# ScalarE copies the finished accumulators out of PSUM, and a memset moves ahead of the first values

## The chip, the cores and the metric

The kernel runs on one core of a Trainium2 chip. The core has a matrix engine (TensorE, PE in the profile, with its weight loads as PEld), three engines for elementwise work (VectorE or DVE, ScalarE or ACT, GpSimd or POOL) and a queue that issues most transfers (SyncE, SP). The metric is the device time of one execution in microseconds (us), of which the median over several runs counts.

## The reference

The input `x` has 8 batches of 3072 rows and 256 columns. The reference takes the Fourier transform over rows and columns, keeps the real part and sends each of the 24576 rows through a small two-layer network:

```
h = real(fft2(x)) @ w_in          # 256 -> 2048
g = max(h, 0) + alpha * min(h, 0) # alpha: one value per hidden unit
y = g @ w_out                     # 2048 -> 256
```

## The kernel before, in words

The transform uses symmetries, so that each batch gives two families of values, kept in a tile `X` of four rows of 1552 columns: row 0 and row 1 hold the high and the low part of one family, rows 2 and 3 those of the other. The functions `unit_store` and `to_x` write `X` (line 592: ACT writes the high part; line 593: POOL or DVE the low part). The buffer of `X` is used earlier in the run by a tile `before`, for input pieces and weights.

The network then works on 26 blocks of columns of `X` (`BLOCKS`, line 28): four of width 386 or 384, eighteen of width 512, four of 386. Each block has 16 steps, one for each 128 hidden units, so there are 416 steps, numbered `s`. `step(s)` (line 795) does, in program order:

- `ffn1(s + 3)`: six first-layer matmuls for the step three ahead, into two of four PSUM banks of the pool `pq`;
- `ffn2(s)`: the second-layer matmuls of this step, twelve once the start is over, into four accumulator banks `acc[o, i]`. `o` is the half of the 256 output columns, `i` one of the two rows that come from one pair of values. The pool `accp` has one buffer for each of the four, so the next block uses the same banks;
- in the last step of a block, `evacuate(g, 0)`: the two banks of half 0 are copied to SBUF and stored;
- `pair(s + 3)`: the activation. DVE adds (`sums`, `row`), ACT makes the product with alpha (line 714), DVE takes the maximum (line 666), ACT rounds to the high part (`hi`, line 668), POOL subtracts for the low part (`lo`, line 670);
- in the last step of a block, `evacuate(g, 1)`: the same for half 1.

The order of `ffn2`'s matmuls is written out. In the last step of a block (line 758) all of half 0 comes first. In all others (line 760) it is half 0 with `woh`, half 0 with `wol`, then half 1 with `wol`, and so on, each for both `i`.

The order of work is written by hand: each engine executes its instructions in the order of the program, and semaphores are set where one instruction needs the result or the place of another. In the first block the steps also prepare the weights (`weights_f`, `weights_b`, `weights_m` on POOL, `weights_mm` on PE), and beside the later steps the transforms and folds of the next batch are made. Input pieces are loaded on SP's queue into a ring of four buffers (`load`, line 186), each as soon as the piece four places ahead of it in the list is used up (`fold_whole`, line 428).

Seven columns behind the last value of `X` are set to zero by a memset on POOL (line 911), after step 3.

Of the kernel before, what the change touches and what calls it, by code (L numbers as in the profile page):

```python
# [9 lines left out]
F32 = mybir.dt.float32  # L10
# [15 lines left out]
XS, X0 = 1552, 7  # L26
SINGLE = 1537
BLOCKS = [(0, 0, 386), (0, 386, 384), (0, 770, 384), (0, 1154, 384)]
# [10 lines left out]
def _halves(v):  # L39

    return v.rearrange("p (h a) -> p a h", h=2)


def _pairs(v):

    return v.rearrange("p (a h) -> p a h", h=2)
# [85 lines left out]
def fft2_prelu_ffn(ctx: ExitStack, tc: tile.TileContext, t, outputs):  # L132
# [17 lines left out]
    V, S, G = nc.vector, nc.scalar, nc.gpsimd  # L150
# [7 lines left out]
    zres = small.tile([P, P], F32, name="zres")  # L158
    before = xp.tile([P, 4, XS], F32, tag="X", name="before")
    dummy = work.tile([P, 512], F32R, tag="hi0", name="dummy", bufs=3)  # L160
# [121 lines left out]
    def weights_m(f, e):  # L282
        a, m = wpart.pop(f)
        w = st.tile([P, 512], F32, tag="w32", name="w32", bufs=2)
        e.tensor_tensor(out=w.bitcast(I32), in0=a, in1=m, op=ALU.add)  # L285
        w32[f] = w
# [239 lines left out]
    def dft(kind, half, fe, fo, zr, m, bank=None):  # L526

        ps = (bank or other_bank())[0:m]
        if kind in TABS:
            tab = TABS[kind]  # L530
            n = 193 if kind[1:] == "ee" else 192
            o = 0 if kind[1:] == "ee" else 3
            even = [(fe[:, o], tab[:, 0]), (fe[:, o + 1], tab[:, 1])]
            if kind == "cee":
                even.append((zr, ee[:, 4]))
            oddp = [(fe[:, o + 1], tab[:, 2]), (fe[:, o + 2], tab[:, 3])]
        else:
            n = 192
            sl = slice(half * 192, (half + 1) * 192)
            even = [(fo[:, q], odd[:, q, sl]) for q in range(3)]  # L540
            oddp = [(fo[:, 3 + q], odd[:, 3 + q, sl]) for q in range(3)]
        for o, terms in ((0, even), (n, oddp)):
            for i, (lhsT, rhs) in enumerate(terms):
                nc.tensor.matmul(  # L544
                    out=ps[:, o:o + n], lhsT=lhsT, rhs=rhs, start=(i == 0), stop=(i == len(terms) - 1),
                )
        return ps, n, m
# [23 lines left out]
    def unit_mm(b, kind, half, bank=None):  # L571
        s = 0 if kind[0] == "c" else 2
        fe, fo = (fold[b, "ce"], fold[b, "co"]) if s == 0 else (fold[b, "se"], fold[b, "so"])
        return dft(kind, half, fe, fo, zres, P, bank)

    def unit_store(b, kind, half, lo_engine, y):
# [9 lines left out]
        if kind == "cee" and 0 < b < NB - 1:  # L586
            c = X0 + SINGLE + b
            lo_engine.tensor_copy(out=X[:, 0:2, c:c + 1], in_=X[:, 0:2, X0:X0 + 1].bitcast(F32))

    def to_x(s, c, v, lo_engine):  # L590
        hi, lo = (X[:, s + i, X0 + c:X0 + c + v.shape[-1]] for i in range(2))
        S.activation(out=hi, in_=v, func=ACTF.Copy)  # L592
        lo_engine.tensor_tensor(out=lo, in0=v, in1=hi.bitcast(F32), op=ALU.subtract)  # L593
# [41 lines left out]
    def column_128_store(kind, y):  # L635
        at, n = _place(1, kind), 385 if kind == "cee" else 384
        nc.sync.dma_start(out=xcd[1:NB, at:at + n], in_=y[1:NB, 0:n])
        at, n = _place(0, kind), y.shape[-1]
        nc.sync.dma_start(out=xcd[0:1, at:at + n], in_=y[0:1])
        if kind == "cee":  # L640
            nc.sync.dma_start(
                out=xcd[NB - 1:NB, SINGLE:SINGLE + 7].rearrange("o (b k) -> (o b) k", k=1), in_=y[0:NB - 1, 0:1],
            )
# [31 lines left out]
    def ffn1(s):  # L675
# [4 lines left out]
        for q in range(2):  # L680
            t_ = pq.tile([P, 512], F32, tag="pq", name="pq")[:, 0:w]
            xh, xl = X[:, 2 * q, c:c + w], X[:, 2 * q + 1, c:c + w]
            xh, xl, out = _halves(xh), _halves(xl), _pairs(t_)
# [54 lines left out]
    acc = {}  # L738
# [34 lines left out]
    def evacuate(g, o):  # L773
        b, c, w = BLOCKS[g]
        if o == 0:
            outs[g] = outp.tile([P, 2, 2, w], F32, tag="o", name="o")
        v = outs[g]
        dst = outputs[g]
        for i in range(2):
            if o == 0:  # L780
                S.activation(out=v[:, o, i], in_=acc[o, i], func=ACTF.Copy)
            else:
                V.tensor_copy(out=v[:, o, i], in_=acc[o, i])
        nc.sync.dma_start(out=dst[:, o], in_=v[:, o])

    outs = {}
# [8 lines left out]
    def step(s):  # L795

        g, f = divmod(s, KF)

        def on(fn, f_, *a):
            if 0 <= f_ < KF:  # L800
                fn(f_, *a)

        if 0 <= s + LEAD < NSTEP:
            ffn1(s + LEAD)
        if s >= 0:
            ffn2(s)
            if f == KF - 1:
                evacuate(g, 0)
        on(weights_mm, s + AHEAD + 1)
        on(weights_ih, s + AHEAD)  # L810

        def early():
            on(weights_c, s + AHEAD)

        def late():
            on(weights_f, s + AHEAD + 3)
            on(weights_b, s + AHEAD + 2)
            on(weights_m, s + AHEAD + 2, G)
            on(weights_out, s + AHEAD + 1)

        if s + LEAD <= NSTEP:
            pair(s + LEAD, early, late)
        if s >= 0 and f == KF - 1:
            evacuate(g, 1)
        for f_ in SPLITS.get(s, ()):
            weights_split(f_)
# [28 lines left out]
    weights_b(1)  # L855
    weights_m(1, G)
    X = xp.tile([P, 4, XS], F32R, tag="X", name="X")
    see_sums = unit_mm(0, "see", 0)
    cee_sums = unit_mm(0, "cee", 0)
    x_sums = odd_sums(*x_sums)  # L860
# [40 lines left out]
    for b in range(NB):  # L901
        mine = [g for g, block in enumerate(BLOCKS) if block[0] == b]
        r_odd, r_fold, r_end = (16, 16, 50) if b == 0 else (0, 4, 36)
        beside = []
        for r in range(len(mine) * KF):
            s = mine[0] * KF + r
            g, f = divmod(s, KF)
            step(s)
            if b == 0:
                if r == 3:  # L910
                    G.memset(X[:, :, X0 + SINGLE:X0 + SINGLE + 7].bitcast(F32), 0.0)  # L911
                    nc.sync.dma_start(out=odd, in_=t["odd"])
                if r == 9:
                    column_128_store("ceo", butterfly(*column_128_mm("ceo", 0)))
                if r in (10, 11):
                    unit(0, ("ceo", "seo")[r - 10], 0, G)
                if r in (12, 13):
                    fold_cross(0, ("co", "so")[r - 12])
                    if r == 13:
                        fold_128(0)  # L920
                if r == 25:
                    start.close()
                    late = ctx.enter_context(tc.tile_pool(name="late", bufs=1))
                if r in TABLE_STEPS:
                    q = TABLE_STEPS.index(r)
                    v = late.tile([P, 1, 384], F32, tag="table", name="table", bufs=2)
                    nc.sync.dma_start(out=v, in_=t["odd"][:, q:q + 1])
                    parts(v, "odd", G, q)
            if f == 10:
                load_xbc(g + 1)  # L930
            q = r - r_odd
            if b == 0 and q in (0, 2, 4, 6):
                unit(b, ("co", "so")[q // 2 % 2], q // 4, G)
            if b and q in (0, 3):
                nm = ("co", "so")[q // 3]
                store_odd(b, nm, dft_odd(b, nm), G)
            if b + 1 < NB:
                if r == r_fold:
                    fold_tiles(b + 1)
                for i, e, r0, r1 in FOLDS:  # L940
                    r0, r1 = (r_fold + round(v * (r_end - r_fold)) for v in (r0, r1))
                    if r == r0:
                        by = one_by_one if e is V else spread
                        beside.append(by(fold_whole(6 * b + 6 + i, e), r0, r1))
                for x in beside:
                    next(x, None)
                if r == r_end + 1:
                    fold_rows(b + 1)
                    fold_cross(b + 1)
                    fold_128(b + 1)  # L950
                for nm, at in (("co", 60), ("so", 62)) if b == 0 else (("co", 44), ("so", 46)):
                    if r == at:
                        parts(fold[b + 1, nm], nm, G)
                for kind, at in zip(("see", "cee", "ceo", "seo"), (53, 55, 57, 58) if b == 0 else (38, 40, 41, 42)):
                    if r == at:
                        unit(b + 1, kind, 0, G)
# [64 lines left out]
```

## Time and profile before

| What | us |
|---|---|
| median of 3 runs (lowest, highest) | 1664.68 (1663.48, 1667.77) |
| the profiled execution | 1664.33 |
| its span in the profile | 1662.5 |
| busy: PE, DVE, POOL, ACT | 1642.7, 1473.8, 1299.3, 1123.8 |
| PE's share of the chain that ended last | 93% |

A busy time says how long an engine executed something. The chain that ended last is followed back from the last instruction, at each step to what released it. In the rows of a timeline the first number is the start in us from the span's start, the second the duration of the merged group, then come engine, line, operation, tiles and the number of instructions; in brackets stands the engine's idle time just before, and what ended it.

### The profile page before, as it was taken

The numbers are of one execution on the slowest core, as the hardware profiler recorded it, in microseconds if no ns is written. First come the engines' busy times: TensorE is split into PE (matmuls) and PEld (weight loads), VectorE is DVE, ScalarE is ACT, GpSimd is POOL, SyncE is SP. The second block draws the span as 40 slices with busy tenths as digits, with TensorE's granted clock in tenths as the row PEclk, the third lists the DMA queues.
The fourth block names the chain that finished last, engine by engine and source line by source line (L and its number), as shares of the span: only waits on it lengthen the run. The fifth ranks groups of instructions, "written<-read, shape, count | busy, mean of one in ns | idle before, by whom it ended". The sixth has DMA issues, their size and how long they took to land.

```text
span 1662.5 us, 26282 instructions
## 1 busy us (share of the span) xinstructions
PE 1642.7 (99%) x8222; PEld 1475.8 (89%) x8222; DVE 1473.8 (89%) x2545; ACT 1123.8 (68%) x2029; POOL 1299.3 (78%) x1349
## 2 busy tenths in 40 slices
PE   8999999999999999999999999999999999999998
PEld 6789899888888888888888888888888888899998
DVE  7888998899889997899978998889988999789997
ACT  5876677666676667666676666766676666677765
POOL 2369888788778887789877897778877888676665
PEclk9999999999999999999999999999999999999999
DMA  6410120011000110010100111001010010000000
GB/s 242 138 63 28 45 88 20 7 70 39 32 26 20 58 52 20 33 39 33 70 1 32 52 33 58 26 7 71 37 35 26 20 45 31 1 31 25 25 20 20
DMA packets 26158, 71.40 MB, mean 43 GB/s; under 512 B 6273, under 2 KB 8355, under 8 KB 25891
## 3 DMA queue, kind: packets, MB, share of 16 engines
q1 hardware_dynamic: 25266, 69.27, 12.0%
q8 instruction: 66, 1.08, 0.3%
q14 instruction: 74, 0.60, 0.1%
q10 hardware_dynamic: 752, 0.45, 0.1%
HBM read 44.45 MB, written 25.25 MB: 42 GB/s over the span
## 4 chain that ended last, share of the span: by engine, by line
PE 93%; DVE 4%; issue 1%; ACT 0%; DMA 0%; POOL 0%; DVEq 0%; SPq 0%; POOLq 0%; ACTq 0%
PE acc L767 56%; PE pq L684 10%; PE pq L685 10%; PE pq L686 10%; PE ps L544 3%; PE ps L498 2%; PE acc L751 2%; DVE d L710 1%; DVE pf L702 1%; PE ps L316 1%; DVE d L666 1%; PE fold L393 0%; DMA raw<-in_xh 0%; DVE wm L276 0%; DVE we L272 0%
## 5 line engine op out<-in xcount | busy, mean ns | idle before, releaser
L670 POOL TENSOR_TENSOR lo<-d,hi 128x512 fp32r<-128x512 f32 (+2 forms) x804 | 972.9, 1227 | 258.6 <-ACT hi L668 247.8
L668 ACT ACTIVATE hi<-d 128x512 fp32r<-128x512 f32 (+2 forms) x804 | 483.2, 601 | 387.9 <-DVE d L666 315.4
L666 DVE SCALAR_TENSOR_TENSOR d<-d,sg,pq 128x512 f32<-128x512 f32 (+2 forms) x804 | 563.8, 701 | 6.7 <-ACT pq L714 6.7
L714 ACT ACTIVATE pq<-d,sga 128x512 f32<-128x512 f32 (+2 forms) x804 | 526.3, 655 | 48.9 <-DVE d L710 48.1
L710 DVE TENSOR_TENSOR d<-pf,pq 128x512 f32<-128x512 f32 (+2 forms) x832 | 529.2, 639 | 7.8
L767 PE MATMUL acc<-hi,woh 128*128 128x512 f32 (+2 forms) x1608 | 454.1, 364 | 0.0
L767 PE MATMUL acc<-lo,woh 128*128 128x512 f32 (+2 forms) x1608 | 393.1, 364 | 0.0
L767 PE MATMUL acc<-hi,wol 128*128 128x512 f32 (+2 forms) x1608 | 393.1, 364 | 0.0
L702 DVE SCALAR_TENSOR_TENSOR pf<-xbc,w,pq 128x512 f32<-128x512 f32 (+2 forms) x416 | 298.3, 717 | 92.6 <-PE pq L686 87.6
L767 PEld LDWEIGHTS acc<-hi,woh 128*128 128x128 f32 x1608 | 298.0, 189 | 31.0
L767 PEld LDWEIGHTS acc<-lo,woh 128*128 128x128 f32 x1608 | 295.3, 189 | 30.9
L767 PEld LDWEIGHTS acc<-hi,wol 128*128 128x128 f32 x1608 | 295.3, 189 | 30.9
L684 PE MATMUL pq<-X,wih 128*128 128x512 f32 (+2 forms) x832 | 310.7, 373 | 7.1 <-DVE d L666 6.5
L685 PE MATMUL pq<-X,wih 128*128 128x512 f32 (+2 forms) x832 | 302.6, 364 | 2.0 <-POOL X L911 1.8
L686 PE MATMUL pq<-X,wil 128*128 128x512 f32 (+2 forms) x832 | 302.5, 364 | 0.0
L684 PEld LDWEIGHTS pq<-X,wih 128*128 128x128 f32 x832 | 157.6, 189 | 26.9 <-PE pq L686 4.1
L685 PEld LDWEIGHTS pq<-X,wih 128*128 128x128 f32 x832 | 157.7, 190 | 17.2 <-POOL X L911 2.1
L686 PEld LDWEIGHTS pq<-X,wil 128*128 128x128 f32 x832 | 157.6, 189 | 15.7 <-DVE wil L333 0.3
L593 POOL TENSOR_TENSOR X<-y,X 128x384 fp32r<-128x384 f32 (+3 forms) x67 | 63.3, 957 | 14.8 <-ACT X L592 14.0
L384 POOL TENSOR_TENSOR raw<-raw 128x512 f32<-128x512 f32 (+2 forms) x84 | 69.5, 827 | 0.0
L285 POOL TENSOR_TENSOR w<-we,wm 128x512 int32<-128x512 int32 x16 | 20.4, 1272 | 51.8 <-DVE wm L276 49.6
L561 DVE TENSOR_TENSOR y<-ps,os 128x192 f32<-128x192 f32 (+3 forms) x76 | 23.5, 352 | 40.4 <-ACT os L551 40.4
(155 smaller groups left out, 988.0 us busy)
## 6 DMA issues: line engine op xcount, KB each, us to landing
raw<-in_xh SPq DMA_DIRECT2D x46, 512.0 KB
out<-o SPq DMA_DIRECT2D x36, 512.0 KB
raw<-in_w SPq DMA_DIRECT2D x15, 512.0 KB
xbc<-xcd SPq DMA_DIRECT2D x18, 256.0 KB
out<-o SPq DMA_DIRECT2D x10, 386.0 KB
out<-o SPq DMA_DIRECT2D x6, 384.0 KB
odd<-in_odd SPq DMA_DIRECT2D x1, 1152.0 KB
table<-in_odd SPq DMA_DIRECT2D x6, 192.0 KB
```

The source lines that it names most:

```text
L384: yield size, lambda o=o, i0=i0, i1=i1, op=op: e.tensor_tensor(out=o, in0=i0, in1=i1, op=op)
L593: lo_engine.tensor_tensor(out=lo, in0=v, in1=hi.bitcast(F32), op=ALU.subtract)
L666: V.scalar_tensor_tensor(out=d, in0=d, scalar=sg[:, f:f + 1], in1=ad, op0=ALU.mult, op1=ALU.max)
L668: S.activation(out=hi, in_=d, func=ACTF.Copy)
L670: G.tensor_tensor(out=lo, in0=d, in1=hi.bitcast(F32), op=ALU.subtract)
L684: nc.tensor.matmul(out=out, lhsT=wih[:, f, q], rhs=xh, start=True, stop=False)
L685: nc.tensor.matmul(out=out, lhsT=wih[:, f, q], rhs=xl, start=False, stop=False)
L686: nc.tensor.matmul(out=out, lhsT=wil[:, f, q], rhs=xh, start=False, stop=True)
L702: V.scalar_tensor_tensor(out=_pairs(pf), in0=_halves(xbc[g]), scalar=w128[:, f:f + 1], in1=_pairs(ps[0]), op0=ALU.mult, op1=ALU.add,)
L710: V.tensor_tensor(out=d, in0=pf, in1=ps[1], op=ALU.add if i else ALU.subtract)
L714: S.activation(out=ad, in_=d, func=ACTF.Copy, scale=sga[:, f:f + 1])
L767: nc.tensor.matmul(out=out, lhsT=wt[:, f, o * P:(o + 1) * P], rhs=rhs, start=(f == 0 and n[o] == 0), stop=(f == KF - 1 and n[o] == 2),)
```

## The change

In `evacuate`, half 1 is no longer copied by DVE but by ACT, as half 0 is; the last block alone keeps DVE for one of its four copies. The place of `evacuate` in the step does not change. The memset of `X` moves from the end of step 3 to the line behind the allocation of `X`.

```diff
         for i in range(2):
-            if o == 0:
+            if g == len(BLOCKS) - 1 and o == i == 1:
+                V.tensor_copy(out=v[:, o, i], in_=acc[o, i])
+            else:
                 S.activation(out=v[:, o, i], in_=acc[o, i], func=ACTF.Copy)
-            else:
-                V.tensor_copy(out=v[:, o, i], in_=acc[o, i])
         nc.sync.dma_start(out=dst[:, o], in_=v[:, o])
...
     X = xp.tile([P, 4, XS], F32R, tag="X", name="X")
+    G.memset(X[:, :, X0 + SINGLE:X0 + SINGLE + 7].bitcast(F32), 0.0)
     see_sums = unit_mm(0, "see", 0)
...
                 if r == 3:
-                    G.memset(X[:, :, X0 + SINGLE:X0 + SINGLE + 7].bitcast(F32), 0.0)
                     nc.sync.dma_start(out=odd, in_=t["odd"])
```

## Rows read from the trace of the kernel before

**Rows 1.** The page: busy us, share of the span and instructions, by engine.

```profile
PE 1642.7 (99%) x8222; PEld 1475.8 (89%) x8222; DVE 1473.8 (89%) x2545; ACT 1123.8 (68%) x2029; POOL 1299.3 (78%) x1349
```

**Rows 2.** Busy time by stretch: length, PE, PEld, DVE, ACT, POOL, granted clock, DMA.

```profile
300.00:1650.00 1350.00, 1350.00 (x6630) 1213.01 (x6629) 1207.31 (x1986) 907.82 (x1577) 1090.40 (x1080) 1.00 0.10 33
```

**Rows 3.** PE's waits from 116 us on: us in total, times, longest.

```profile
PE pq L684 <- DVE d L666: 5.9, 8, 2.3
```

**Rows 4.** DVE's copies (line 783): count, ns min/median/max, first and last start.

```profile
L783 DVE COPY o<-acc x52: 542/678/693, 115.7 to 1658.4; 128x512 f32<-128x512 f32 x36, 128x386 f32<-128x386 f32 x10, 128x384 f32<-128x384 f32 x6
```

**Rows 5.** Timeline of DVE at the boundary from block 8 to 9.

```profile
608.45 1.28 DVE L783 COPY o<-acc 128x512 f32<-128x512 f32 x2
609.65 0.75 DVE L702 SCALAR_TENSOR_TENSOR pf<-xbc,w,pq 128x512 f32<-128x512 f32 x1
```

**Rows 6.** Timeline of PE at the same boundary, block 9's first second-layer matmuls.

```profile
609.59 0.59 PE L767 MATMUL acc<-hi,woh 128*128 128x512 f32 x2
610.02 1.03 PE L767 MATMUL acc<-hi,wol 128*128 128x512 f32 x4
```

**Rows 7.** Timeline of DVE after block 1.

```profile
174.03 1.01 DVE L783 COPY o<-acc 128x384 f32<-128x384 f32 x2
...
180.45 3.52 DVE L384 TENSOR_TENSOR xev<-raw 128x512 f32<-128x512 f32 x1 [0.20 <-DMA raw<-in_xh]
```

**Rows 8.** Timeline of ACT at the boundary from block 8 to 9.

```profile
606.99 1.08 ACT L781 ACTIVATE o<-acc 128x512 f32<-128x512 f32 x2 [1.55 <-PE acc L767]
...
609.61 0.69 ACT L714 ACTIVATE pq<-d,sga 128x512 f32<-128x512 f32 x1
611.17 0.63 ACT L668 ACTIVATE hi<-d 128x512 fp32r<-128x512 f32 x1 [0.87 <-DVE d L666]
```

**Rows 9.** Timeline of PE around the memset, with the next two steps' beginnings.

```profile
60.15 0.41 PE L684 MATMUL pq<-X,wih 128*128 128x386 f32 x1
62.38 0.43 PE L685 MATMUL pq<-X,wih 128*128 128x386 f32 x1 [1.83 <-POOL X L911]
62.65 0.33 PE L686 MATMUL pq<-X,wil 128*128 128x386 f32 x1
...
66.71 0.41 PE L684 MATMUL pq<-X,wih 128*128 128x386 f32 x1
...
71.17 0.41 PE L684 MATMUL pq<-X,wih 128*128 128x386 f32 x1
```

**Rows 10.** Timeline of POOL, the memset of X.

```profile
62.20 0.13 POOL L911 MEMSET X<- 128x28 f32 x1
```

**Rows 11.** Timeline of ACT at the end of block 24, width 386.

```profile
1614.90 0.59 ACT L714 ACTIVATE pq<-d,sga 128x386 f32<-128x386 f32 x1
```

**Rows 12.** Timeline of all engines at the end of the run.

```profile
1656.99 0.88 ACT L781 ACTIVATE o<-acc 128x386 f32<-128x386 f32 x2 [2.60 <-PE acc L767]
...
1657.61 0.49 PE L767 MATMUL acc<-lo,woh 128*128 128x386 f32 x2
...
1657.97 1.03 DVE L783 COPY o<-acc 128x386 f32<-128x386 f32 x2 [4.22 <-PE acc L767]
```

**Rows 13.** Timeline of PE, block 25's first second-layer matmuls.

```profile
1614.73 0.49 PE L767 MATMUL acc<-hi,woh 128*128 128x386 f32 x2
1615.06 0.82 PE L767 MATMUL acc<-hi,wol 128*128 128x386 f32 x4
```

**Rows 14.** Timeline of POOL where the memset goes.

```profile
25.65 0.19 POOL L328 MEMSET wih<- 1x128 f32 x1
```

**Rows 15.** Timeline of ACT, DVE and PE at the first writes into X.

```profile
25.45 0.53 ACT L592 ACTIVATE X<-y 128x386 fp32r<-128x386 f32 x1 [1.03 <-DVE y L561]
25.88 0.32 ACT L551 ACTIVATE os<-ps 128x193 f32<-128x193 f32 x1
26.23 0.62 DVE L561 TENSOR_TENSOR y<-ps,os 128x193 f32<-128x193 f32 x2
27.46 0.43 PE L684 MATMUL pq<-X,wih 128*128 128x386 f32 x1 [0.55 <-ACT X L592]
```

## The prediction

> **What bounds the kernel now.** I read the shares of the page first: TensorE (PE) is busy 99% of the span, VectorE (DVE) 89%, ScalarE (ACT) 68% [rows 1]. An average over stages can mislead, so the busy time of one long stretch comes next: from 300 to 1650 us PE is busy 1350.00 of 1350.00 us at a granted clock of 1.00, DVE 1207 and ACT 908 [rows 2]. There PE never stops; whatever another engine saves in that stretch is worth nothing, and whatever makes PE stop is lost in full. Third, the list of PE's waits: from 116 us to the end PE waits for DVE only, 8 times, 5.9 us together, 2.3 us the longest [rows 3]. None of these falls between 300 and 1650 us [rows 2]. So there is little to gain in the steady part, and the start, before 116 us, is the only place with waits that an edit of this size can remove.
>
> **Part 1: 50 copies go from VectorE to ScalarE.** Before, each of the 26 blocks is copied out by two ACT copies (half 0) and two DVE copies (half 1): 52 of each, median 678 ns on DVE [rows 4]. After, ACT does all four in 25 blocks and three in the last.
>
> What DVE gets back: 50 x 0.68 = 34 us of work, and none of it is on the path. At the boundary that I follow (block 8 to block 9, widths 512) DVE starts the two copies at 608.45, ends them at 609.73, and begins the next step's first operation at 609.65 [rows 5], while PE runs without a gap [rows 6]. I take 0 for it; the bound on the other side is the 5.9 us of [rows 3], less the 2.3 us wait that follows a DVE operation of 3.52 us on a freshly loaded x piece [rows 7], which no copy causes: 3.6 us.
>
> What ACT takes on: the program order on its queue is two copies of half 0, then hi, product, hi, product of the pair, and only then, from line 824, the copies of half 1. In the block shown ACT starts the half-0 copies at 606.99, as soon as PE has finished these banks, and runs to the second product at 609.61, which ends at 610.30; the next instruction, at 611.17, had waited 0.87 us [rows 8]. The new copies fit ACT's gap nearly exactly: they start about 610.22, if neighbours overlap by 0.08 us as DVE's do (609.73 against 609.65 [rows 5]), and last 1.08 us for both, to 611.30. ACT itself is not made late by more than 0.1 us. But the accumulator banks have one buffer each, and the next block needs them earlier. Its first step of second-layer matmuls goes to half 0 four times and then, in the order of line 760, to half 1: the fifth and sixth matmul. The first two start at 609.59, the next four at 610.02, 0.216 us apart [rows 6], so the fifth starts at 610.45 and the sixth at 610.67. DVE had the banks free at 609.73. ACT frees the second at 611.30, and 0.05 us pass until PE goes on (62.33 to 62.38 after the memset [rows 9, 10]). The sixth matmul therefore starts at 611.35 and not at 610.67: 0.68 us lost, in two pieces (about 0.40 and 0.28). PE's queue is in order, so nothing passes the waiting matmul: behind it stand the rest of the step and the next step's first-layer matmuls, and behind those everything else.
>
> 18 boundaries lead into a block of width 512: 18 x 0.68 = 12.2 us. The other 7 lead into a block of 384 or 386. There the second product ends at 1614.90 + 0.59 = 1615.49 [rows 11]; less 0.08, plus two copies in 0.88 us (the pair in [rows 12]), plus 0.05, PE may go on at 1616.34; the sixth matmul stood at 1615.06 + 3 x 0.163 = 1615.55 [rows 13]: 0.79 us, 7 x 0.79 = 5.5 us. Together 17.7 us.
>
> A matmul that has waited is also followed late: after the memset's wait the next one came 0.27 us later [rows 9] against the 0.163 of width 384 and 386. This adds 0.05 (0.27 - 0.216) at width 512 and 0.11 at the narrow ones if it happens once a boundary: 18 x 0.05 + 7 x 0.11 = 1.7 us; it could be 0, if only the matmul and not its weights waits, or twice that. I take 1.7: 19.4 us.
>
> I take one of these as absorbed. The boundary after block 1, whose copies begin at 174.03, lies some 6 us ahead of PE's 2.3 us wait, which hangs on the load that DVE needs at 180.45 [rows 3, 7]; by lines 188 and 430 that load waits for GpSimd (POOL) to finish an earlier piece, not for PE. Its 0.9 us is taken off: 18.5 us. If nothing is absorbed it is 19.4; if the seven other waits of [rows 3] absorb as well, up to 3.6 us less.
>
> What else moves: the store of half 1 is issued about 1.6 us later on SP's queue, and the x pieces' loads stand behind it; they are issued a ring of four ahead, several steps before use, so 0. In block 0 two weight splits on ACT (line 826) come 0.9 us later, and are used a step later still, 0.
>
> *Rules weighed.* The Trainium skill (Perfetto Trace Analysis, section Optimizing Scalar/DVE Operations) says that with a saturated VectorE some of its work may well be given to ScalarE. By it alone DVE's relief would be the gain; by [rows 2] it is worth nothing here, since PE and not DVE is full. The same page (Matmuls) wants independent groups to rotate through banks so that evacuation of one overlaps the next; that speaks against this change. Taken alone it would put a stall in the kernel before as well, and [rows 6] show none: what counts is whether the copy ends before the fifth matmul.
>
> **Part 2: the memset.** At line 911 it stands in POOL's queue behind a weight operation. Its region spans all four rows of X, and the matmul that reads row 1 waits for it though no column is shared: 1.83 us idle until 62.38, while the one on row 0 went at 60.15 [rows 9]; the memset itself runs at 62.20 for 0.13 us [rows 10]. The step that holds it takes 66.71 - 60.15 = 6.56 us, the next 71.17 - 66.71 = 4.46 [rows 9]: 2.10 us go. What would be late next in that step is the usual chain of its neighbours, hence their 4.46.
>
> In its new place the memset follows weight 1's operation on POOL, at 25.65, where a small memset starts today [rows 14], and ends at 25.78. By the same spanning region ACT's first write into X, today at 25.45 [rows 15], has to wait for it: to about 25.83, 0.38 us. Queued behind it on ACT is the copy at 25.88, for which DVE's operation at 26.23 waits, and behind that the first matmul at 27.46 [rows 15]. I take +0.38, the other bound being 0 if the first write isn't held.
>
> **Part 3: the last block.** Today both DVE copies run one after the other, 1657.97 to 1659.00 [rows 12]. After, ACT copies one (1657.97 to about 1658.46) and DVE the other: its matmul is the second of the pair at 1657.61, 0.16 us later, so 1658.13 + 0.56 = 1658.69. The store goes 0.31 us earlier; 0 at worst.
>
> **Sum** against the profiled execution, 1664.33 us (span 1662.5 and 1.8 around it): + 18.5 - 2.10 + 0.38 - 0.31 = + 16.5, so 1680.8 us. The median of the runs is 0.35 us higher; on it, 1681.2 us.
>
> **Rivals.**
> *No stall (ends not slower).* If the half-1 copies ended before the fifth matmul, at 610.45 [rows 6], only parts 2 and 3 count: 1664.7 - 2.0 = 1662.7 us. It decides at 0.68 us on ACT: the second product would have to end at 609.62 instead of 610.30 for both copies to be in time. For it speaks only that ACT has 32% to spare; against it that this chain on ACT begins with a wait of 1.55 us for PE [rows 8], so that it cannot start sooner: the half-0 banks are ready no earlier.
> *DVE's relief is what counts.* Up to the 3.6 us of waits above go as well: with no stalls 1664.7 - 2.0 - 3.6 = 1659.1 us. PE full for 1350 us [rows 2] speaks against it. The Trainium skill's rule on a saturated VectorE, above, would lead here.
> *The stall is longer.* If ACT, now late, is also late for the next step's hi parts, each boundary costs both whole copies, 1.09 us: 25 x 1.09 = 27, so about 1690 us. The gap of 0.87 us against 1.08 us of work speaks for a part of it.
> *Half a stall.* If PE loses only the first of the two pieces, 25 x 0.4 = 10 us, about 1672.7 us.
>
> **How the numbers follow.** Forecast 0.72, longer stall 0.08, half a stall 0.08, no stall 0.09, DVE's relief 0.03. The forecast's own range is 1675 to 1684 (0 to 3.4 us for the matmuls that follow late, 0 to 4.5 us absorbed). To leave out no more than 2 in 10 I go to 1671 and 1688. A measurement of this kernel can tell about 0.3% from no change, which is 5 us. Slower comes from the forecast, the longer and the half stall: 0.88. Same is no stall, 0.09, and faster is DVE's relief, 0.03.
>
> **What would show it.** In the timeline after: the second product, then two ACT copies back to back with no gap; PE idle before the fifth and the sixth matmul of each block but the first, put down to ACT's copy, some 0.7 us at each of the 25 boundaries, in up to 50 waits; PE below 1350 in 300 to 1650. DVE's share falls by 2 points and changes nothing. No PE wait at 62 us; the first write into X waits for the memset. I am wrong if PE has no wait for ACT's copies, or if it has them and the span doesn't grow with their sum.

## The result, and the profile after

The changed kernel takes 1679.95 us (median of 6 runs, 1678.65 to 1681.46) against 1664.85 us for the kernel before (6 runs, 1663.48 to 1667.77): ratio 1.0088, 95% interval 1.0075 to 1.0101 (ratios here and below are worked out from the single runs, so they differ a little from those of the medians). By the medians it is 15.1 us slower; 16.5 were forecast.

The page after, busy us by engine (before: [rows 1]):

```profile
PE 1654.2 (99%) x8222; PEld 1474.3 (88%) x8222; DVE 1442.6 (86%) x2494; ACT 1142.6 (68%) x2080; POOL 1299.0 (77%) x1349
```

and its stretch from 300 to 1650 us, columns as in [rows 2]:

```profile
300.00:1650.00 1350.00, 1344.08 (x6526) 1194.89 (x6526) 1168.38 (x1917) 911.44 (x1596) 1077.69 (x1068) 1.00 0.10 33
```

In the same 1350 us PE executed 6526 matmuls and not 6630, at the same clock. DVE is relieved, 1473.8 to 1442.6 us, and PE is not full any more.

The waits after from 116 us on, those of PE (us in total, times, longest):

```profile
PE acc L767 <- ACT o L783: 7.0, 24, 0.4
PE pq L684 <- DVE d L666: 3.4, 6, 1.1
```

and those of its weight loads:

```profile
PEld acc L767 <- ACT o L783: 22.8, 49, 0.8
```

The wait for ACT's copy (line 783 is now ACT's) is new. PE's row shows 7.0 us of it and the weight loads' row 22.8. The matmuls' ends are modelled, so a short stop between two of them partly vanishes in PE's busy time. What the stop costs is read from starts: take the same matmul in both traces, and watch where the distance between them changes.

The boundary from block 8 to block 9 after, on ACT (before: [rows 8]):

```profile
608.65 1.09 ACT L783 ACTIVATE o<-acc 128x512 f32<-128x512 f32 x2 [1.55 <-PE acc L767]
...
611.27 0.69 ACT L714 ACTIVATE pq<-d,sga 128x512 f32<-128x512 f32 x1
611.89 1.08 ACT L783 ACTIVATE o<-acc 128x512 f32<-128x512 f32 x2
612.84 0.64 ACT L668 ACTIVATE hi<-d 128x512 fp32r<-128x512 f32 x1
```

and on PE (before: [rows 6]):

```profile
611.26 0.59 PE L767 MATMUL acc<-hi,woh 128*128 128x512 f32 x2
611.69 0.59 PE L767 MATMUL acc<-hi,wol 128*128 128x512 f32 x2
612.53 0.97 PE L767 MATMUL acc<-hi,wol 128*128 128x512 f32 x2 [0.25 <-ACT o L783]
613.34 0.59 PE L767 MATMUL acc<-hi,woh 128*128 128x512 f32 x2
```

Half 1's copies stand directly behind the second product. The fifth matmul was due at 611.69 + 2 x 0.216 = 612.12 and started at 612.53, 0.41 late; the seventh was due at 612.55 and started at 613.34, 0.79 late. The weight loads there:

```profile
612.53 0.19 PEld L767 LDWEIGHTS acc<-hi,wol 128*128 128x128 f32 x1 [0.65 <-ACT o L783]
613.02 0.19 PEld L767 LDWEIGHTS acc<-hi,wol 128*128 128x128 f32 x1 [0.30 <-ACT o L783]
613.13 0.41 PEld L767 LDWEIGHTS acc<-hi,woh 128*128 128x128 f32 x2
```

The waiting matmul's weights wait with it: the sixth's load only at 613.02, 0.05 after the copies end (612.97). So the next matmul can't follow at the usual 0.216: 613.34 - 613.02 = 0.32.

DVE's waits for PE between 300 and 1650 us, in the kernel before:

```profile
DVE pf L702 <- PE pq L686: 79.1, 200, 1.0
```

and after:

```profile
DVE pf L702 <- PE pq L686: 114.8, 247, 1.4
```

They grow by 35.7 us. That is close to the 34 us of all copies that DVE has lost, but it does not show what the relief is worth. In this stretch DVE has 42 copies fewer, 27.8 us by their durations, and it also stands still while PE is stopped. In experiment 4, with the same copies gone and PE not stopped, these waits are 85.8 us. The worth of the relief has to be read from the times of the runs there.

At the memset's old place, PE after (before: [rows 9]):

```profile
60.10 0.41 PE L684 MATMUL pq<-X,wih 128*128 128x386 f32 x1
60.34 0.33 PE L685 MATMUL pq<-X,wih 128*128 128x386 f32 x1
...
64.56 0.41 PE L684 MATMUL pq<-X,wih 128*128 128x386 f32 x1
```

No wait, and the step takes 4.46 us instead of 6.56: 2.10 less. At its new place, on POOL (before: [rows 14]):

```profile
25.55 0.12 POOL L858 MEMSET X<- 128x28 f32 x1
```

on ACT (before: [rows 15]):

```profile
25.35 0.53 ACT L592 ACTIVATE X<-y 128x386 fp32r<-128x386 f32 x1 [1.04 <-DVE y L561]
```

on PE:

```profile
27.40 0.43 PE L684 MATMUL pq<-X,wih 128*128 128x386 f32 x1 [0.58 <-ACT X L592]
```

ACT's first write started 0.20 us before the memset: it did not wait for it. The first matmul is not later than before (27.46).

The end, on ACT (before: [rows 12]):

```profile
1672.27 1.47 ACT L783 ACTIVATE o<-acc 128x386 f32<-128x386 f32 x3 [2.60 <-PE acc L767]
```

on DVE:

```profile
1673.42 0.56 DVE L781 COPY o<-acc 128x386 f32<-128x386 f32 x1 [4.38 <-PE acc L767]
```

on PE:

```profile
1672.89 0.49 PE L767 MATMUL acc<-lo,woh 128*128 128x386 f32 x2
```

The last copy ends 1673.98 - 1672.89 = 1.09 us after the last pair of matmuls began; before it was 1659.00 - 1657.61 = 1.39. The 0.31 is there; behind it this execution took 4.1 us to the end of its span, the one before 3.5.

**Where the time went**, from the starts of the first first-layer matmul of each step in both profiles (a stretch is named by the step of `ffn1` that it ends at): the 25 boundaries add 20.4 us (0.78 or 0.79 each between two wide blocks, 17 times; 0.84 from the narrow block 3 into the wide block 4; 0.80 to 0.94 into the seven narrow ones, mostly 0.89); the memset's step gives back 2.10; the four steps from 37 to 40, around 180 us, give back 2.8; the other steps together give back about 0.2. That makes + 15.3 at the last step. The two profiled times differ by 1679.9 - 1664.33 = 15.6.

### The profile page after: what moved, and what is told of

The parts are those of the page before. It is cut to its first block, busy times and chain, and to the rows that moved or that the text cites. A ratio compares the mean times of both kernels' runs of the same rounds, so it can differ in the third digit from the quotient of the medians.

```text
span 1678.1 us, 26265 instructions
## 1 busy us (share of the span) xinstructions
PE 1654.2 (99%) x8222; PEld 1474.3 (88%) x8222; DVE 1442.6 (86%) x2494; ACT 1142.6 (68%) x2080; POOL 1299.0 (77%) x1349
## 3 DMA queue, kind: packets, MB, share of 16 engines
q8 instruction: 66, 1.08, 0.3%
## 4 chain that ended last, share of the span: by engine, by line
PE 90%; ACT 5%; DVE 3%; issue 2%; POOL 0%; DMA 0%; DVEq 0%; ACTq 0%; POOLq 0%
PE acc L767 54%; PE pq L684 9%; PE pq L686 9%; PE pq L685 9%; PE ps L544 3%; PE ps L498 2%; PE acc L751 2%; ACT pq L714 2%; ACT o L783 2%; ACT hi L668 1%; PE ps L316 1%; DVE d L710 1%; DVE d L666 1%; DVE pf L702 1%; PE fold L393 0%
## 5 line engine op out<-in xcount | busy, mean ns | idle before, releaser
L767 PE MATMUL acc<-hi,wol 128*128 128x512 f32 (+2 forms) x1608 | 405.9, 367 | 7.5 <-ACT o L783 7.3
L593 POOL TENSOR_TENSOR X<-y,X 128x384 fp32r<-128x384 f32 (+3 forms) x67 | 63.2, 956 | 20.4 <-ACT X L592 19.9
L783 ACT ACTIVATE o<-acc 128x512 f32<-128x512 f32 (+2 forms) x103 | 52.5, 564 | 29.9 <-PE acc L767 29.7
```

Source lines behind the costliest of these rows:

```text
L767: nc.tensor.matmul(out=out, lhsT=wt[:, f, o * P:(o + 1) * P], rhs=rhs, start=(f == 0 and n[o] == 0), stop=(f == KF - 1 and n[o] == 2),)
```

## The experiments

**1. The copies without the memset's move.** `evacuate` as changed, the memset left in step 3. Against the changed kernel:

```
-    G.memset(X[:, :, X0 + SINGLE:...], 0.0)      # behind X's allocation
...
+                    G.memset(X[:, :, X0 + SINGLE:...], 0.0)   # if r == 3
```

> The copies go to ScalarE, the memset stays behind step 3. Theory (the half-1 banks come free too late, about 0.79 us per boundary into a wide block and 0.89 into a narrow one): 20.4 us at the 25 boundaries, less what earlier waits absorb, so 16 to 20 us slower than before, 1681 to 1685 us, with the 1.8 us wait for the memset still there. Rival (the loss needs the earlier start that the moved memset gives): less than 10 us slower.

Measured: 1682.6 us (1680.41 to 1683.78; before on this chip 1664.48), ratio 1.011, interval 1.0089 to 1.0131. The boundaries cost the same 0.79 and 0.89 us, and the memset's wait is in PE's list before 116 us:

```profile
PE pq L685 <- POOL X L911: 2.5, 1, 2.5
```

The copies alone carry the loss; the memset has no part in it.

**2. The memset's move without the copies.** Against the kernel before:

```
+    G.memset(X[:, :, X0 + SINGLE:...], 0.0)      # behind X's allocation
...
-                    G.memset(X[:, :, X0 + SINGLE:...], 0.0)   # if r == 3
```

> Only the memset moves; VectorE copies as before. Theory: the step with the memset falls from 6.56 to 4.46 us and nothing is lost at the first writes, so 2.1 us faster, 1662.7 us; if the 3.5 us VectorE operation at 180 us goes as well, some 2.5 us more. No wait of the matrix engine at a block boundary. Rival (ScalarE's first write is held by 0.38 us): 1.7 us faster.

Measured: 1661.37 us (1658.90 to 1663.85), ratio 0.9983, interval 0.9971 to 0.9995: 2.8 us by the ratio. The memset's step is 2.10 us shorter and no boundary waits. The start is 0.11 us later (27.57 for the first matmul), not 0.38. In the four profiles with the memset at its old place the first matmul starts at 27.19 to 27.46, in the six with it moved at 27.19 to 27.66, so no delay of that size shows. In this profile steps 37 to 40 are 1.9 us shorter too, which has another cause (below); the move itself is the 2.10, a small gain.

**3. The next block's first step with all of half 0 first.** The copies' place stays; what needs half 1's banks comes two matmuls later.

```
-        if f == KF - 1:
+        if f in (0, KF - 1):
```

> The changed kernel, but in the first step of a block all six matmuls of half 0 come ahead of those of half 1, so that the half-1 banks are needed two matmuls later (0.43 us at width 512, 0.33 at 384 and 386). Theory (the copy's end against the matmul's due time): the loss per boundary falls by just that, from 0.79 to 0.36 and from 0.89 to 0.56 us, about 10 us in all; 1669 to 1671 us. Rival (the loss comes from ScalarE being late for the next step's work): no change, 1680 us.

Measured: 1669.72 us (1666.92 to 1672.01), ratio 1.0032, interval 1.002 to 1.0044. Each wide boundary costs 0.36 us (0.41 into block 4), most narrow ones 0.57 (0.47 to 0.62). The boundary on ACT:

```profile
611.33 1.07 ACT L783 ACTIVATE o<-acc 128x512 f32<-128x512 f32 x2
```

on PE:

```profile
611.56 0.59 PE L767 MATMUL acc<-lo,woh 128*128 128x512 f32 x2
611.99 0.95 PE L767 MATMUL acc<-hi,woh 128*128 128x512 f32 x2
612.78 0.59 PE L767 MATMUL acc<-hi,wol 128*128 128x512 f32 x2
```

and the weight loads' wait from 116 us on:

```profile
PEld acc L767 <- ACT o L783: 13.1, 49, 0.4
```

ACT does the same work in the same order; PE's deadline alone has moved, by 0.43 us, and the loss falls by 0.43 (at the narrow boundaries the use moved by 0.33 and the loss fell by 0.32). An ACT that is late for the next step's parts would cost the same as before. So the price is the copy's end against the bank's next use.

**4. The same four copies, but half 1's directly behind half 0's,** ahead of `pair`; the rest as in the changed kernel.

```
                 evacuate(g, 0)
+                evacuate(g, 1)
...
-        if s >= 0 and f == KF - 1:
-            evacuate(g, 1)
```

> The changed kernel, but ScalarE's half-1 copies stand right behind its half-0 copies, ahead of the pair's hi and product. Theory (only the place in ScalarE's queue costs): the copies end about 609.5 on the scale of the boundary after block 8, before the fifth matmul; no wait at the boundaries; the hi parts and products come 1.5 us later and still in time. So as with the memset alone, 1660 to 1663 us, although VectorE has 34 us less to do. Rival 1 (VectorE's relief is worth something once the stall is gone): below 1660 us. Rival 2 (the pair's delay on ScalarE turns into a new wait for VectorE's maximum and the pq banks): 1668 us or more.

Measured: 1660.72 us (1659.79 to 1661.85), ratio 0.9978, interval 0.9968 to 0.9987: faster than both kernels. The boundary on ACT:

```profile
602.50 1.09 ACT L783 ACTIVATE o<-acc 128x512 f32<-128x512 f32 x2 [1.55 <-PE acc L767]
603.80 1.09 ACT L783 ACTIVATE o<-acc 128x512 f32<-128x512 f32 x2 [0.21 <-PE acc L767]
604.77 0.63 ACT L668 ACTIVATE hi<-d 128x512 fp32r<-128x512 f32 x1
```

on PE:

```profile
605.54 1.03 PE L767 MATMUL acc<-hi,wol 128*128 128x512 f32 x4
```

and the stretch from 300 to 1650 us:

```profile
300.00:1650.00 1350.00, 1350.00 (x6630) 1212.39 (x6629) 1190.63 (x1946) 928.77 (x1620) 1086.59 (x1080) 1.00 0.09 33
```

DVE's waits in that stretch, for PE and for ACT's product:

```profile
DVE pf L702 <- PE pq L686: 85.8, 211, 1.0
DVE d L666 <- ACT pq L714: 17.7, 40, 0.7
```

and for the product in the kernel before:

```profile
DVE d L666 <- ACT pq L714: 5.5, 19, 0.6
```

The copies end at 604.89, the fifth matmul comes at about 605.97, and PE is full again. DVE waits longer for the products, which now come two copies later; PE feels that at four of the seven narrow boundaries alone, 0.18 or 0.19 us each, one step behind the boundary. These runs show no part of the copies in the gain over the kernel before: with the memset moved alone (experiment 2) the ratio is 0.9983, and the intervals overlap. ACT executes the same instructions here as in the changed kernel, so its load was never the price; their place in its queue was.

**5. The first of half 1's copies done twice,** which adds one copy to the queue and leaves out nothing.

```
+                if o == 1 and i == 0 and g < len(BLOCKS) - 1:
+                    S.activation(out=v[:, o, i], in_=acc[o, i], func=ACTF.Copy)
                 S.activation(out=v[:, o, i], in_=acc[o, i], func=ACTF.Copy)
```

> The changed kernel, but ScalarE copies the first of the two half-1 banks twice in each block but the last, so that the second bank comes free one copy later (0.49 us at width 512, 0.40 at 384 and 386). Theory (each us by which the copy ends later is a us of the whole run): 18 x 0.49 + 7 x 0.40 = 11.6 us more than the changed kernel, 1.28 and 1.29 us per boundary, about 1691.5 us. Rival (part of it is paid back, since the matrix engine's lateness gives the others time): less than 6 us more.

Measured: 1694.59 us (1693.62 to 1696.02), ratio 1.0167, interval 1.015 to 1.0184. A wide boundary costs 1.42 us. ACT there:

```profile
618.06 0.59 ACT L784 ACTIVATE o<-acc 128x512 f32<-128x512 f32 x1
618.68 1.08 ACT L785 ACTIVATE o<-acc 128x512 f32<-128x512 f32 x2
```

on PE:

```profile
619.33 0.97 PE L767 MATMUL acc<-hi,wol 128*128 128x512 f32 x2 [0.88 <-ACT o L785]
```

The second copy reads the same bank and writes the same place as the first. It starts 0.62 us after it, 0.03 behind its end (618.06 + 0.59 = 618.65), and its record in the trace has a wait for ACT's own earlier instruction, which the other copies here have not. Two copies of different banks to different places overlap and start 0.49 apart (1.08 for both, 0.59 for one). The expectation had taken 0.49, hence its miss of 3 us. The loss grew by 1.42 - 0.79 = 0.63 at a wide boundary and by 1.42 - 0.89 = 0.53 at most narrow ones: whatever lengthens the chain on ACT is paid in full at each of the 25.

**6. The kernel before with its memset cut into four,** one for each row of `X`, at the old place.

```
-                    G.memset(X[:, :, X0 + SINGLE:...], 0.0)
+                    for q in range(4):
+                        G.memset(X[:, q, X0 + SINGLE:...], 0.0)
```

> The kernel before, but the memset behind step 3 is four memsets, one for each row of X. Theory (the matmul on row 1 waited because the one memset's region spans from row 0 to row 3, though it shares no column): no wait of the matrix engine at 62 us, the step takes 4.5 us, and the run 2 us less than before. Rival (any memset of X at that place is waited for): the wait stays and grows by the three memsets, 0.3 us.

One run: 1661.91 us (before 1665.81 on this chip). On PE:

```profile
59.54 0.41 PE L684 MATMUL pq<-X,wih 128*128 128x386 f32 x1
59.79 0.33 PE L685 MATMUL pq<-X,wih 128*128 128x386 f32 x1
```

on POOL:

```profile
61.70 0.22 POOL L912 MEMSET X<- 128x7 f32 x4
```

The read of row 1 went 1.9 us ahead of the memsets. It had waited for a region that spans the rows, not for a value.

**7. The kernel before with one POOL fold moved,** to see whether the long DVE operation at 180 us depends on what POOL does beside it.

```
-    FOLDS = (..., (3, G, 0.5, 0.75), ...)
+    FOLDS = (..., (3, G, 0.53, 0.75), ...)
```

> The kernel before, but GpSimd begins its third x piece of batch 1 one step later (0.53 for 0.5 in the table of folds), so that its first operation on it no longer stands at 182.1 us. Theory (VectorE's 3.52 us operation at 180.45 was held by GpSimd's operations, the last of which ended 0.55 us before it): the operation takes less than 2.6 us and the matrix engine's wait behind it shrinks by the same. Rival (it waited for its load): 3.5 us as before.

One run: 1662.4 us. The operation took 1.35 us and not 3.52, and PE gained 2.2 us there. By itself this proves little: it is also short in kernels whose fold is at the old place (0.75 in experiment 4). Inconclusive.

**8. The kernel before with the memset moved and only the last block's copies shared,** so that DVE keeps the other 25 blocks.

```
-            if o == 0:
+            if o == 0 or g == len(BLOCKS) - 1 and i == 0:
```

> The memset moved, VectorE copies half 1 as before, but in the last block ScalarE takes one of its two copies. Theory: as with the memset alone, and the last copy ends 0.3 us sooner after the last matmul: 0.92 us instead of 1.23; about 1661 us. Against the kernel with ScalarE's copies early it shows what VectorE's relief is worth: nothing, within 1 us. Rival: the early copies stay faster by more than 2 us.

Measured: 1661.93 us (1658.66 to 1664.24), ratio 0.998, interval 0.9971 to 0.9989. Its end on PE:

```profile
1654.82 0.49 PE L767 MATMUL acc<-lo,woh 128*128 128x386 f32 x2
```

on DVE:

```profile
1655.34 0.56 DVE L783 COPY o<-acc 128x386 f32<-128x386 f32 x1 [4.38 <-PE acc L767]
```

The last copy ends 1.08 us after the last pair began, 0.31 sooner than before. Against experiment 4 (0.9978) it is the same within both intervals: with the stall gone, 34 us less work on DVE buys nothing that these runs can tell.

## Why the prediction was right, point by point

- **The place and the mechanism** held: half 1's copies directly behind the second product, the fifth and sixth matmul waiting, all behind them in PE's queue late. Experiments 3, 4 and 5 move the bank's next use, the copies, and the chain's length, and the loss follows each. The rivals *no stall* and *half a stall* fall with the 0.79 us of a boundary; *the stall is longer* with ACT's next `hi`, which starts as soon as the copies let it, and with experiment 3.
- **The size of a boundary**: 0.68 + 0.05 = 0.73 forecast at width 512, 0.79 measured; 0.79 + 0.11 = 0.90 at the narrow ones, 0.89 measured. The sixth matmul, due at 611.69 + 3 x 0.216 = 612.34, starts with its weights' load at 613.02: the 0.68 late that were forecast. The late follower is real (0.32 between sixth and seventh start); its 0.05 was half of what it is, 0.10, since it was taken from one wait at width 386 [rows 9]. Over all, 20.4 us against 19.4.
- **DVE's relief** at nothing: right (experiment 4 against 2 and 8).
- **The memset's** 2.10: right to the hundredth. The **+0.38 for a held first write** was wrong: the write into row 2 started 0.20 us before the memset in the changed kernel, and as much in the five experiments that move it. A read inside the spanned region was held [rows 9], and set free by experiment 6; a write inside it was not. Why the two differ no run here shows.
- **The last block's** 0.31: right (after, and experiment 8).
- **The "absorbed" 0.9 us was the wrong step.** It put the DVE operation of 3.52 us at 180.45 [rows 7] down to a load. After, the operation on the same piece is this, on DVE:

```profile
179.10 0.99 DVE L384 TENSOR_TENSOR xev<-raw 128x512 f32<-128x512 f32 x1
```

The boundary ahead of it paid its 0.89 in full; nothing was absorbed. What went, with steps 37 to 40, is the operation's own length: 3.52 - 0.99 = 2.53 of the 2.8 us. Against the kernel before, these steps are 1.9 to 2.9 us shorter in all six profiles where the operation is short, and 0.7 to 1.3 longer in the three others where it is long. Where it is long, POOL's operations beside it run back to back at their usual pace, as before on POOL, beside the DVE operation from 180.45 to 183.97:

```profile
180.22 1.98 POOL L670 TENSOR_TENSOR lo<-d,hi 128x384 fp32r<-128x384 f32 x2
182.14 1.28 POOL L384 TENSOR_TENSOR xeg<-raw 128x512 f32<-128x512 f32 x1
```

and in experiment 8 on DVE:

```profile
176.89 3.64 DVE L384 TENSOR_TENSOR xev<-raw 128x512 f32<-128x512 f32 x1
```

on POOL:

```profile
176.79 1.97 POOL L670 TENSOR_TENSOR lo<-d,hi 128x384 fp32r<-128x384 f32 x2
178.72 1.26 POOL L384 TENSOR_TENSOR xeg<-raw 128x512 f32<-128x512 f32 x1
```

In both it ends 0.55 us behind POOL's third operation (183.97 against 183.42, 180.53 against 179.98). In all ten profiles it ends 0.54 to 0.56 us behind the end of a POOL operation; where it is short, that is the one that ran when it began. After, POOL is the one that is held up:

```profile
178.54 2.41 POOL L670 TENSOR_TENSOR lo<-d,hi 128x384 fp32r<-128x384 f32 x2
180.92 1.28 POOL L384 TENSOR_TENSOR xeg<-raw 128x512 f32<-128x512 f32 x1
```

Its pair takes 2.41 and not 1.98: DVE got in between. In ten profiles the operation took 0.75 to 1.38 us six times and 3.36 to 3.64 four times, with DVE's copies (before, experiments 6 and 8: long; 2 and 7: short) and with ACT's (experiment 3: long; after, 1, 4, 5: short). So both lengths come with either engine's copies; whether the change shifts the odds, ten profiles can't tell. What decides it stays open: it starts 0.10 to 0.43 us into POOL's pair where it is long, and 0.17 to 0.66 us into it in five of the short ones (0.16 ahead of it in experiment 4). It is 2 to 3 us of a comparison of two single profiles, and why single runs of the kernel before lie as far apart as 1660.53 and 1667.77 may in part be this; that wasn't shown.

The errors nearly cancel: + 1.0 on the stall, + 0.9 not absorbed, - 0.4 for the write, - 2.8 around 180 us, + 0.6 behind the last copy, and - 0.2 in other steps make - 0.9, from 16.5 to the 15.6 of the profiles. The sum is right in its large terms, and partly by luck in the small ones. The small gains of steps 22 and 53 (0.29, 0.24) were not traced. Step 57 is 0.68 us longer, as it is by 0.65 to 1.30 in experiments 1, 3, 4 and 5, all with ACT's copies; in the kernels with DVE's copies it is 0.19 at most. In the profiles with ACT's copies PE waits there for DVE's maximum ahead of a transform's matmul (line 544; 0.51 us after), which it doesn't with DVE's. This is a small loss that comes with the copies and that the prediction did not have; why was not tested.

## What to carry to other kernels

When a copy out of PSUM goes to a less loaded engine, don't count load: find the end of the copy in that engine's order and the start of the next matmul into the same bank, and take the difference, times the boundaries. If it is positive, move the copy ahead of work that nobody is waiting for yet (here one line, from 0.88% slower to 0.22% faster), or the bank's next use back. In that 0.22% the copies have no share that these runs can tell: the memset's move alone gives 0.17%. And a wait seen once in one profile, as the one at 180 us, is no cover to subtract until its cause is known.

## What was not expected of the hardware

- A DVE operation with both inputs in SBUF took 0.75 us in one profile and 3.64 in another. The Trainium skill (SBUF — State Buffer, section Who interferes with whom) says that such an operation contends with a GpSimd instruction that reads SBUF, and that the order of issue decides who blocks. The trace agrees in part: in six profiles the operation ended 0.55 us behind the one POOL operation that ran when it began, and POOL's next took 1.43 to 1.46 us instead of about 1.0. In the other four it had begun ahead of POOL's next two operations, and yet ended behind both, 3.36 to 3.64 us after its start.
- A matmul that waits for its bank keeps its weights waiting too in this kernel (22.8 us on the weight loads, 7.0 on the matmuls; the sixth matmul's load at 613.02), so that the one behind it is 0.10 us later than the pace at width 512.
